# Eight PSUM banks and six in front for the second products of a feed-forward layer

## The chip, the cores and the metric

One core of a Trainium2 chip runs the whole program as one launch. The metric is the device time of that launch in microseconds. The engines are TensorE (PE, with its weight loads as PEld), VectorE (DVE), ScalarE (ACT), GpSimd (POOL) and SyncE (SP, which issues most of the DMAs).

## The reference, cut to what matters

Attention in a window, then a mixture of eight experts over all tokens, then one feed-forward layer. The change touches the last of these:

```python
def _moe2_ref(x, w_in, w_out):              # x 2304 x 512, w_in 512 x 2048, w_out 2048 x 512
    h = x @ w_in
    g = np.where(h >= 1, h, np.where(h <= -1, 0.0, (h + 1) ** 2 / 4))
    return g @ w_out
```

## The kernel before

Each fp32 product is made of three matmuls on a high and a low part of both factors (`mm3`, lines 76 to 78). The feed-forward layer is done with Strassen's scheme: seven block products in place of eight, for both matrix products.

The tokens go in three phases of 768. In each phase the 2048 inner columns go in eight units of 256, two units at a time. For a pair (i, i+1) the program first runs `g1` for both units and then one call of `g2s`.

`g1` makes the seven first products of a unit in four PSUM tiles with the tags a, b, c and d (one buffer each). Its last piece of work is a list of steps, `put7`, on ACT, DVE and POOL: it applies the activation g to the four quarters c22, f11, c21 and c12 of the result, forms the sums s13 and s24 of them (POOL, lines 726 to 732), and splits the seven blocks into `hh` (high, ACT, line 705) and `hl` (low, DVE, line 708). The blocks are numbered 0 to 6 in this order: c22, f11, c12, the two of s13 (3, 4), the two of s24 (5, 6). One step of every open list is given out at each "tick", so the order of the instructions in each engine's queue is the order in which the ticks gave them out, and each engine works its queue off in that order. The steps of the second unit's put7 are still being given out while g2s runs.

`g2s` makes the seven second products for three 128-token tiles: 21 results of 128 x 256. Two results share one PSUM bank (2 KB), so there are eleven "banks" of work, 0 to 10, block by block (bank 0 holds block 0 of tiles 0 and 1, bank 3 block 2 of tiles 0 and 1, bank 10 block 6 of tile 2). Each gets a first part from unit i and a second part from unit i+1. A full part is 6 matmuls, that of bank 10 is 3, so a call has 126. After its second part a bank is drained: in the first pair of a phase ACT copies it into the accumulator `acf` (line 842), in the others DVE adds it there (line 844). A tick comes after every third result part. The last call of the program takes the banks in another order, which starts with the blocks 0 and 1 and has blocks 5 of tile 0 in its bank 5.

The banks rotate through four PSUM buffers, which have the tag g2. Four first parts go in front; then come the second part of bank 0, the second part of bank 1, the first part of bank 4, the second part of bank 2, the first part of bank 5, and so on. The order is written out by the loop at the end of g2s:

```python
for b in range(4):
    yield from bank(b, 0)
for b in range(len(banks)):
    yield from bank(b, 1)
    drain(b)
    if 1 <= b < len(banks) - 3:
        yield from bank(b + 3, 0)
```

Behind the last call the three tiles are combined and stored (`combine`, lines 805 and 800, and lines 850 and 854).

Of the kernel before, what the change touches and what calls it, by code (L numbers as in the profile page):

```python
# [11 lines left out]
F32 = mybir.dt.float32  # L12
# [7 lines left out]
P = 128  # L20
# [9 lines left out]
def attn_moe_ffn(ctx: ExitStack, tc, q, k, v, w_gate, w1, w2, w_in, w_out, out):  # L30
# [10 lines left out]
    FU = 2 * P  # L41
# [33 lines left out]
    def mm3(ps, lh, ll, rh, rl, first, last, on=False):  # L75
        nc.tensor.matmul(ps, lhsT=lh, rhs=rh, start=first, stop=False, skip_group_check=on)  # L76
        nc.tensor.matmul(ps, lhsT=lh, rhs=rl, start=False, stop=False, skip_group_check=on)  # L77
        nc.tensor.matmul(ps, lhsT=ll, rhs=rh, start=False, stop=last, skip_group_check=on)  # L78
# [498 lines left out]
    def is_first(i):  # L577
        return i == 0 or units[i][:2] != units[i - 1][:2]

    def is_last(i):  # L580
        return i == NU - 1 or units[i][:2] != units[i + 1][:2]
# [207 lines left out]

    BLOCK = (6, 0, 1, 3, 5, 4, 2)  # L790
    NB = TH // P

    def combine(t, ns, acc, engines):

        n0, n1 = ns[0], ns[-1] + 1
        a = [acc[:, n0:n1, s, :] for s in range(7)]

        def put(s, r, x):
            rows_ = t * TP + r * TH
            nc.sync.dma_start(out=out[rows_ + n0 * P:rows_ + n1 * P, x * FU:(x + 1) * FU].rearrange("(n p) d -> p n d", p=P),  # L800
                              in_=a[s])

        for n, (o, x, z) in enumerate(((5, 1, None), (0, 4, None), (3, 5, None), (2, 1, (0, 0)), (6, 3, (0, 1)),
                                       (0, 5, (1, 0)), (3, 4, (1, 1)))):
            engines[n % len(engines)].tensor_tensor(a[o], a[o], a[x], ALU.add)
            if z is not None:
                put(o, *z)
            yield

    def g2s(i, acc, psp):  # L810

        kind, t, e, j = units[i]
        ops = [[*HT.pop(u), *W2.pop(u)] for u in (i, i + 1)]
        first, last = is_first(i), is_last(i + 1)
        end = i + 2 == NU
        flat = acc.rearrange("p n s d -> p (n s) d")
        if end:
            order = [(0, 0), (0, 1), (1, 0), (1, 1), (0, 2), (1, 2), (0, 3), (0, 4), (1, 3), (1, 4), (0, 5), (0, 6),
                     (1, 5), (1, 6), (2, 0), (2, 1), (2, 3), (2, 5), (2, 2), (2, 4), (2, 6)]
        else:  # L820
            order = [(n, s) for s in range(7) for n in range(NB)]
        banks = [sorted(order[x:x + 2]) for x in range(0, len(order), 2)]
        PS = {}
        count = [0]

        def part(b, x, u):
            if x == 0 and u == 0:
                PS[b] = psp.tile([P, 2, FU], F32, tag="g2", bufs=4, name="psg2")
            n, s = banks[b][x]
            hh, hl, wh, wl = ops[u]  # L830
            ts = slice(n * P, (n + 1) * P)
            mm3(PS[b][:, x], hh[:, s, ts], hl[:, s, ts], wh[:, BLOCK[s]], wl[:, BLOCK[s]], u == 0 and x == 0, u == 1,
                True)
            count[0] += 1
            return count[0] % 3 == 0

        def drain(b):
            f = [n * 7 + s for n, s in banks[b]]
            a = flat[:, f[0]:f[-1] + 1:max(f[-1] - f[0], 1)]
            ps = PS.pop(b)[:, 0:len(f)]  # L840
            if first:
                nc.scalar.activation(a, ps, AF.Copy)
            else:
                nc.vector.tensor_tensor(a, ps, a, ALU.add)  # L844

        V, G = nc.vector, nc.gpsimd
        n2 = [acc[:, NB - 1, s, :] for s in range(7)]

        def add(eng, o, x):
            eng.tensor_tensor(n2[o], n2[o], n2[x], ALU.add)  # L850

        def store(s, r, x):
            r0 = t * TP + r * TH + (NB - 1) * P
            nc.sync.dma_start(out=out[r0:r0 + P, x * FU:(x + 1) * FU], in_=n2[s])

        def bank(b, u):
            for x in range(len(banks[b])):
                if part(b, x, u):
                    yield

        for b in range(4):
            yield from bank(b, 0)
        for b in range(len(banks)):
            yield from bank(b, 1)
            drain(b)
            if 1 <= b < len(banks) - 3:
                yield from bank(b + 3, 0)
            if end:
                if b in (5, 6):
                    post.append(combine(t, [b - 5], acc, (V, G)))  # L870
                elif b == 8:
                    add(V, 5, 1)
                    add(V, 3, 5)
                    add(G, 6, 3)
                elif b == 9:
                    add(G, 0, 4)
                    add(G, 0, 5)
                    store(0, 1, 0)
                elif b == 10:
                    store(6, 0, 1)  # L880
                    add(V, 3, 4)
                    store(3, 1, 1)
                    add(V, 2, 1)
                    store(2, 0, 0)
        if last and not end:
            post.append(combine(t, list(range(NB)), acc, (V, G)))

# [79 lines left out]
    with tc.manual_schedule():  # L967
# [218 lines left out]
        for i in range(0, NU, 2):  # L1186
# [6 lines left out]
            if i and kind > units[i - 1][0]:  # L1193
# [4 lines left out]
                accp, hop, wp2 = (ctx.enter_context(tc.tile_pool(name=n, bufs=1)) for n in ("acf", "hpf", "w2f"))  # L1198
                acc = accp.tile([P, NB, 7, FU], F32, name="acf")
                pools["hop"] = hop  # L1200
# [20 lines left out]
            if kind == 0:  # L1221
                run(g2(i, acc, ps2, stg), False)
            else:
                run(g2s(i, acc, ps2), False)
                if i + 8 < NU and is_first(i):
                    side.append(sums(phase(i + 8)))
# [32 lines left out]
```

## Time and profile before

| | |
|---|---|
| three runs | 2120.49, 2121.81 and 2129.6 us; median 2121.81 |
| profiled execution | 2124.34 us, span 2122.6 |
| mean granted clock of PE | 0.988 of full speed |
| PE busy | 2051.3 us (97%) |
| DVE busy | 1342.4 us (63%) |
| ACT busy | 746.0 us (35%) |
| POOL busy | 727.2 us (34%) |
| DMA, mean over the span | 234 GB/s |

Matmuls overlap in the profile (the next starts before the last has ended), so a busy PE isn't PE at its peak; how densely they start says more. The feed-forward layer fills the last 420 us or so of the span, with twelve calls of g2s.

### The profile page before, as it was taken

The numbers are of one execution on the slowest core, as the hardware profiler recorded it, in microseconds if no ns is written. First come the engines' busy times: TensorE is split into PE (matmuls) and PEld (weight loads), VectorE is DVE, ScalarE is ACT, GpSimd is POOL, SyncE is SP. The second block draws the span as 40 slices with busy tenths as digits, with TensorE's granted clock in tenths as the row PEclk, the third lists the DMA queues.
The fourth block names the chain that finished last, engine by engine and source line by source line (L and its number), as shares of the span: only waits on it lengthen the run. The fifth ranks groups of instructions, "written<-read, shape, count | busy, mean of one in ns | idle before, by whom it ended". The sixth has DMA issues, their size and how long they took to land.

```text
span 2122.6 us, 32070 instructions
## 1 busy us (share of the span) xinstructions
PE 2051.3 (97%) x11719; PEld 1869.4 (88%) x11719; DVE 1342.4 (63%) x2967; ACT 746.0 (35%) x1716; POOL 727.2 (34%) x755
## 2 busy tenths in 40 slices
PE   7999999999999999999999999999999999898987
PEld 5888888998999898999899888899899889898987
DVE  5766655554555756666667656666666566858676
ACT  5767343333333331221122221121122263555542
POOL 4333346666756401112111011111110045646333
PEclk9999999999999999999999999999999999999998
DMA  7333568776777787676677597676675685775852
GB/s 152 82 86 96 196 222 328 246 263 247 254 252 258 261 324 260 235 258 230 237 266 249 192 339 244 232 275 226 229 273 208 224 315 197 307 280 208 320 196 100
DMA packets 238797, 496.91 MB, mean 234 GB/s; under 512 B 70704, under 2 KB 152624, under 8 KB 238640
## 3 DMA queue, kind: packets, MB, share of 16 engines
q1 hardware_dynamic: 222640, 475.34, 63.5%
q10 hardware_dynamic: 16000, 19.53, 3.0%
q8 instruction: 92, 1.51, 0.3%
q14 instruction: 65, 0.53, 0.1%
HBM read 353.39 MB, written 141.03 MB: 233 GB/s over the span
## 4 chain that ended last, share of the span: by engine, by line
PE 82%; DVE 6%; ACT 5%; DMA 4%; issue 1%; SPq 1%; POOL 0%; DVEq 0%; ACTq 0%; POOLq 0%
PE psg L76 15%; PE psg L78 14%; PE psg L77 14%; PE psc L76 3%; PE psd L76 3%; PE psc L77 3%; PE psc L78 3%; PE psd L77 3%; PE psd L78 3%; PE psb L76 2%; PE psb L78 2%; PE psb L77 2%; PE psa L77 2%; PE psa L78 2%; PE psa L76 2%; PE pso L375 2%
## 5 line engine op out<-in xcount | busy, mean ns | idle before, releaser
L76 PE MATMUL psg<-w2h,hh 128*128 128x512 f32 (+1 forms) x1584 | 574.5, 363 | 38.5 <-DVE acf L844 28.2
L78 PE MATMUL psg<-w2h,hl 128*128 128x512 f32 (+1 forms) x1584 | 571.2, 361 | 0.1
L77 PE MATMUL psg<-w2l,hh 128*128 128x512 f32 (+1 forms) x1584 | 570.9, 360 | 0.2 <-DMA w2l<-wd2l 0.2
L76 PEld LDWEIGHTS psg<-w2h,hh 128*128 128x128 f32 x1584 | 307.3, 194 | 82.5 <-DVE acf L844 30.4
L912 DVE SCALAR_TENSOR_TENSOR acc<-psg,pt,acc 128x512 f32<-128x512 f32 x252 | 187.8, 749 | 253.5 <-PE psg L78 252.0
L78 PEld LDWEIGHTS psg<-w2h,hl 128*128 128x128 f32 x1584 | 306.9, 194 | 42.9 <-DVE hl L708 0.5
L77 PEld LDWEIGHTS psg<-w2l,hh 128*128 128x128 f32 x1584 | 307.5, 194 | 40.4 <-DMA w2l<-wd2l 0.4
L684 ACT ACTIVATE hh<-c 128x384 fp32r<-128x384 f32 x270 | 140.8, 521 | 90.4 <-DVE c L779 53.9
L686 DVE SCALAR_TENSOR_TENSOR hl<-c,hh 128x384 fp32r<-128x384 f32 x270 | 164.0, 640 | 0.0
L751 ACT ACTIVATE p<-psa 128x384 f32<-128x384 f32 x57 | 28.0, 491 | 381.8 <-PE psa L78 353.0
L76 PE MATMUL psd<-sh,w1h 128*128 128x384 f32 x456 | 154.5, 339 | 2.2 <-DVE c L767 1.7
L78 PE MATMUL psd<-sh,w1l 128*128 128x384 f32 x456 | 153.4, 336 | 0.0
L77 PE MATMUL psd<-sl,w1h 128*128 128x384 f32 x456 | 153.3, 336 | 0.0
L192 POOL TENSOR_TENSOR t<-e 128x128 f32<-128x128 f32 x32 | 15.1, 471 | 380.4 <-DVE e L168 380.4
L193 POOL TENSOR_TENSOR t<-e,t 128x128 f32<-128x128 f32 x32 | 15.5, 484 | 324.2 <-DVE e L168 324.2
L726 POOL TENSOR_TENSOR s<-c,c 128x384 f32<-128x384 f32 x24 | 30.3, 1263 | 270.0 <-DVE c L702 270.0
L82 POOL TENSOR_TENSOR w2l<-raw,w2h 128x512 fp32r<-128x512 f32 x60 | 81.7, 1383 | 116.6 <-ACT w2h L81 116.6
L343 POOL TENSOR_TENSOR s<-s,mx 128x512 f32<-128x512 f32 (+2 forms) x80 | 66.6, 848 | 124.4 <-DVE mx L341 67.5
L76 PE MATMUL psc<-x0h,w1h 128*128 128x384 f32 x272 | 92.8, 341 | 2.3 <-DVE u L764 2.3
L761 DVE TENSOR_TENSOR u<-psb,p 128x384 f32<-128x384 f32 x57 | 31.7, 556 | 99.8 <-PE psb L78 79.6
L78 PE MATMUL psc<-x0h,w1l 128*128 128x384 f32 x272 | 92.4, 340 | 0.0
L77 PE MATMUL psc<-x0l,w1h 128*128 128x384 f32 x272 | 92.4, 340 | 0.0
(273 smaller groups left out, 4742.8 us busy)
## 6 DMA issues: line engine op xcount, KB each, us to landing
w1h<-wd1h SPq DMA_DIRECT2D x84, 896.0 KB, 4.8
w1l<-wd1l SPq DMA_DIRECT2D x84, 896.0 KB, 7.5
raw<-in_moe_w SPq DMA_DIRECT2D x60, 512.0 KB, 4.5
w2h<-wd2h SPq DMA_DIRECT2D x60, 512.0 KB, 5.4
w2l<-wd2l SPq DMA_DIRECT2D x60, 512.0 KB, 6.3
wd1h<-w1h SPq DMA_DIRECT2D x30, 896.0 KB, 6.2
wd1l<-w1l SPq DMA_DIRECT2D x30, 896.0 KB, 6.5
w2h<-wd2h SPq DMA_DIRECT2D x28, 896.0 KB, 7.2
```

Source lines behind the costliest of these rows:

```text
L76: nc.tensor.matmul(ps, lhsT=lh, rhs=rh, start=first, stop=False, skip_group_check=on)
L77: nc.tensor.matmul(ps, lhsT=lh, rhs=rl, start=False, stop=False, skip_group_check=on)
L78: nc.tensor.matmul(ps, lhsT=ll, rhs=rh, start=False, stop=last, skip_group_check=on)
L82: eng.tensor_tensor(l, x, h.bitcast(F32), ALU.subtract)
L343: nc.gpsimd.tensor_tensor(s[:, 0:nj, :nk], s[:, 0:nj, :nk], mx[:, 6:6 + nj].unsqueeze(2).to_broadcast([P, nj, nk]), ALU.mult)
L375: nc.tensor.matmul(PS[hs, x, :nq], lhsT=nat[b, "v", kb][:n, (2 * hp + j) * D:(2 * hp + j + 1) * D], rhs=at[:n, c, 0, TAIL[j]] if i == FULL ...
L684: nc.scalar.activation(h, c, AF.Relu)
L686: V.scalar_tensor_tensor(l, c, 0.0, h.bitcast(F32), ALU.max, ALU.subtract)
L726: G.tensor_tensor(s13[:, 0], c21, c22, ALU.add)
L751: nc.scalar.activation(p1, pa, AF.Copy)
L761: V.tensor_tensor(u2, pb, p1, ALU.add)
L912: nc.vector.scalar_tensor_tensor(a, ps, sc, a, ALU.mult, ALU.add)
```

## The change

The banks 4 to 7 of a call now take the tags a, b, c and d, which g1 uses before and after; the banks 0 to 3 and 8 to 10 keep the four buffers of g2. So the eleven banks rotate through all eight PSUM banks. Six first parts go in front in place of four, and the first part of bank b + 6 follows the second part of bank b from b = 0 on.

```diff
     NB = TH // P
+    AHEAD = 6
...
             if x == 0 and u == 0:
-                PS[b] = psp.tile([P, 2, FU], F32, tag="g2", bufs=4, name="psg2")
+                tag = {"tag": "abcd"[b - 4]} if 4 <= b < 8 else {"tag": "g2", "bufs": 4}
+                PS[b] = psp.tile([P, 2, FU], F32, name="psg2", **tag)
...
-        for b in range(4):
+        for b in range(AHEAD):
             yield from bank(b, 0)
         for b in range(len(banks)):
             yield from bank(b, 1)
             drain(b)
-            if 1 <= b < len(banks) - 3:
-                yield from bank(b + 3, 0)
+            if b + AHEAD < len(banks):
+                yield from bank(b + AHEAD, 0)
```

PE's queue in the second pair of the first phase: `psg_17952` is bank 0, `psg_17959` bank 1, `psg_18019` bank 4 (before). The rows begin in the second part of bank 1.

```order
L78 MATMUL psg_17959<-w2h,hl 128x256
L76 MATMUL psg_17959<-w2h,hh 128x256
L77 MATMUL psg_17959<-w2l,hh 128x256
L78 MATMUL psg_17959<-w2h,hl 128x256
L76 MATMUL psg_18019<-w2h,hh 128x256
L77 MATMUL psg_18019<-w2l,hh 128x256
```

With the change `psg_18010` is bank 5, `psg_18026` bank 6. The rows begin at the end of bank 5's first part.

```order
L77 MATMUL psg_18010<-w2l,hh 128x256
L78 MATMUL psg_18010<-w2h,hl 128x256
L76 MATMUL psg_17952<-w2h,hh 128x256
L77 MATMUL psg_17952<-w2l,hh 128x256
L78 MATMUL psg_17952<-w2h,hl 128x256
L76 MATMUL psg_17952<-w2h,hh 128x256
```

Before, the first part of bank 4, which takes the buffer of bank 0, was the seventh part and followed two second parts; with the change bank 5's first part stands ahead of the first second part, and the first bank that takes the buffer of bank 0 is bank 8, the eleventh part.

DVE's queue in the same call, from the hl of the first unit's s24 on (`s_17838`); `s_17925` and `s_17926` are s13 and s24 of the second unit, `c_17923` is its c12. Before:

```order
L708 TENSOR_TENSOR hl<-s_17838,hh 128x768
L708 TENSOR_TENSOR hl<-c_17923,hh 128x384
L844 TENSOR_TENSOR acf<-psg_17952,acf 128x2x256
L844 TENSOR_TENSOR acf<-psg_17959,acf 128x2x256
L708 TENSOR_TENSOR hl<-s_17925,hh 128x768
L844 TENSOR_TENSOR acf<-psg_17976,acf 128x2x256
L844 TENSOR_TENSOR acf<-psg_17993,acf 128x2x256
L708 TENSOR_TENSOR hl<-s_17926,hh 128x768
L844 TENSOR_TENSOR acf<-psg_18019,acf 128x2x256
```

With the change (line 846 is the drain that was line 844):

```order
L708 TENSOR_TENSOR hl<-s_17838,hh 128x768
L708 TENSOR_TENSOR hl<-c_17923,hh 128x384
L846 TENSOR_TENSOR acf<-psg_17952,acf 128x2x256
L708 TENSOR_TENSOR hl<-s_17925,hh 128x768
L846 TENSOR_TENSOR acf<-psg_17959,acf 128x2x256
L708 TENSOR_TENSOR hl<-s_17926,hh 128x768
L846 TENSOR_TENSOR acf<-psg_17976,acf 128x2x256
L846 TENSOR_TENSOR acf<-psg_17993,acf 128x2x256
```

The two hl of the second unit's sums moved forward: one drain stands ahead of the first of them in place of two, and two ahead of the second in place of four.

ACT's queue in the first call of the first phase, where ACT drains; `s_17216` and `s_17217` are the second unit's sums. Before:

```order
L705 ACTIVATE hh<-c_17214 128x384
L842 ACTIVATE acf<-psg_17243 128x2x256
L705 ACTIVATE hh<-s_17216 128x768
L842 ACTIVATE acf<-psg_17250 128x2x256
L842 ACTIVATE acf<-psg_17267 128x2x256
L705 ACTIVATE hh<-s_17217 128x768
L842 ACTIVATE acf<-psg_17283 128x2x256
```

With the change:

```order
L705 ACTIVATE hh<-c_17214 128x384
L705 ACTIVATE hh<-s_17216 128x768
L844 ACTIVATE acf<-psg_17243 128x2x256
L705 ACTIVATE hh<-s_17217 128x768
L844 ACTIVATE acf<-psg_17250 128x2x256
L844 ACTIVATE acf<-psg_17267 128x2x256
```

Here too the hh of both sums moved forward, and the drains of banks 1 and 2 now stand behind the hh of s24.

## Rows read from the trace of the kernel before

**Rows 1.** Waits of PE, 1700 us to the end: total us, times, longest.

```profile
PE psg L76 <- DVE acf L844: 28.2, 9, 3.2
PE psg L76 <- ACT acf L842: 7.0, 4, 2.6
```

**Rows 2.** Windows in one ordinary call: length, engines' busy time (instructions), PEclk, DMA share.

```profile
core 0: us, PE busy (x) PEld busy (x) DVE busy (x) ACT busy (x) POOL busy (x), PEclk, DMA share, GB/s
1740.88:1745.20 4.32, 4.32 (x37) 4.27 (x36) 3.93 (x8) 3.99 (x8) 1.49 (x2) 1.00 0.78 267
...
1749.00:1751.40 2.40, 2.40 (x13) 2.40 (x13) 1.62 (x2) 0.85 (x1) 2.40 (x2) 0.50 0.00 0
```

**Rows 3.** Window of the g1 pair ahead of that call.

```profile
1726.17:1740.88 14.71, 14.71 (x86) 14.71 (x85) 9.53 (x17) 9.60 (x19) 5.21 (x4) 1.00 0.92 368
```

**Rows 4.** Windows of the eight ordinary calls of g2s, two of them and the sum.

```profile
1740.88:1761.01 20.13, 16.96 (x127) 16.59 (x127) 15.72 (x22) 7.59 (x13) 16.26 (x16) 0.92 0.29 99
...
1916.00:1934.50 18.50, 15.38 (x128) 15.18 (x128) 15.05 (x22) 6.49 (x11) 13.27 (x12) 1.00 0.31 107
...
sum 159.64, PE 134.34 PEld 132.34 DVE 123.22 ACT 58.37 POOL 95.26; mean PE 16.79 PEld 16.54 DVE 15.40 ACT 7.30 POOL 11.91
```

**Rows 5.** Windows of the three calls that open a phase, two and the sum.

```profile
1708.70:1726.17 17.47, 15.61 (x127) 15.21 (x127) 9.19 (x12) 11.45 (x21) 5.63 (x5) 1.00 0.79 314
1848.00:1866.42 18.42, 15.70 (x127) 15.26 (x127) 9.01 (x13) 12.26 (x23) 6.23 (x5) 1.00 1.04 398
...
sum 55.71, PE 48.40 PEld 47.15 DVE 27.27 ACT 36.02 POOL 18.08; mean PE 16.13 PEld 15.72 DVE 9.09 ACT 12.01 POOL 6.03
```

**Rows 6.** Windows of the last call and of what follows it.

```profile
2089.45:2110.67 21.22, 18.29 (x127) 17.85 (x126) 16.22 (x25) 6.54 (x11) 7.18 (x7) 0.84 0.00 1
2110.67:2122.60 11.93, 0.16 (x2) 0.00 (x0) 6.95 (x11) 0.00 (x0) 5.82 (x7) 0.62 0.40 132
```

**Rows 7.** Timeline of PE: start, duration, line, idle time before and releaser.

```profile
1748.52 0.58 PE L76 MATMUL psg<-w2h,hh 128*128 128x256 f32 x1 [3.17 <-DVE acf L844]
```

**Rows 8.** Timeline of DVE in the same call (T = 1740.88).

```profile
1742.96 0.55 DVE L719 TENSOR_TENSOR c<-psd,u 128x384 f32<-128x384 f32 x1
...
1745.65 1.74 DVE L708 TENSOR_TENSOR hl<-s,hh 128x768 fp32r<-128x768 f32 x1
1747.32 0.55 DVE L708 TENSOR_TENSOR hl<-c,hh 128x384 fp32r<-128x384 f32 x1
1747.79 1.27 DVE L844 TENSOR_TENSOR acf<-psg,acf 128x512 f32<-128x512 f32 x2
1748.99 1.64 DVE L708 TENSOR_TENSOR hl<-s,hh 128x768 fp32r<-128x768 f32 x1
```

**Rows 9.** DMA issues, 1700 us to the end: count, KB each, median us to landing.

```profile
w2h<-wd2h SPq DMA_DIRECT2D x26, 896.0 KB, 7.2
```

**Rows 10.** Timeline of POOL and ACT in the same call.

```profile
1748.80 1.01 POOL L732 TENSOR_TENSOR s<-c,s 128x384 f32<-128x384 f32 x1
...
1749.84 0.85 ACT L705 ACTIVATE hh<-s 128x768 fp32r<-128x768 f32 x1 [2.38 <-POOL s L732]
```

**Rows 11.** Line 708, 1700 us to the end: ns min/median/max, first and last start.

```profile
L708 DVE TENSOR_TENSOR hl<-s,hh x48: 948/1518/1766, 1706.9 to 2103.2; 128x768 fp32r<-128x768 f32 x48
```

**Rows 12.** Timeline of PE and ACT, first two phase-opening calls (T = 1708.70, 1848.00).

```profile
1714.58 0.39 PE L76 MATMUL psg<-w2h,hh 128*128 128x256 f32 x1 [1.41 <-ACT acf L842]
...
1718.22 0.84 ACT L705 ACTIVATE hh<-s 128x768 fp32r<-128x768 f32 x1 [1.31 <-POOL s L732]
...
1719.60 0.39 PE L76 MATMUL psg<-w2h,hh 128*128 128x256 f32 x1 [0.45 <-ACT acf L842]
...
1854.88 0.60 ACT L842 ACTIVATE acf<-psg 128x512 f32<-128x512 f32 x1 [0.93 <-DMA out<-acf]
...
1858.13 0.84 ACT L705 ACTIVATE hh<-s 128x768 fp32r<-128x768 f32 x1 [0.27 <-POOL s L732]
```

**Rows 13.** Timeline of DVE and SP, the last call (T = 2089.45) and its tail.

```profile
2094.23 1.74 DVE L708 TENSOR_TENSOR hl<-s,hh 128x768 fp32r<-128x768 f32 x1
...
2116.72 3.36 SPq L800 DMA_DIRECT2D out<-acf  x7
```

## The prediction

> **What bounds the kernel now.** I read the waits of TensorE (PE) first, then the stretches of the feed-forward second products as windows, then the timeline of one pair of units on every engine that PE waits for.
>
> PE is nearly always busy, so a gain has to come from its few waits or from its clock. The waits [rows 1] show one kind that repeats: the first matmul of a psg bank waits 9 times for a DVE drain (28.2 us) and 4 times for an ACT drain (7.0 us). That is 35.2 us, all in twelve calls of g2s. I write T for the start of a call. A call is 126 matmuls of 256 columns. They run at 0.12 us each: 36 of them fill the 4.32 us of the first window of [rows 2]. So a call needs 126 x 0.12 = 15.12 us, and the g1 pair ahead of it takes 14.71 us [rows 3].
>
> The windows show what the calls take: 159.64 us for the eight ordinary ones [rows 4], 55.71 for the three that open a token phase, whose drains are ACT's [rows 5], 21.22 for the last [rows 6]. That is 236.57 against 12 x 15.12 = 181.4: 55.1 us over. It has two parts. One is the wait itself, in the sample pair 3.17 us [rows 7]. The other is the clock: after that wait PE runs for a while at a granted clock of 0.50, that is 1.2 instead of 2.4 GHz [rows 2]; a matmul then takes 256/1.2 = 0.213 us, 0.093 more. The ordinary call that kept its clock took 18.50 us, 3.4 over the floor, which is wait and restart; its sister at 0.92 took 20.13 [rows 4]. So a wait of some 3 us costs about 1.5 us more in clock, mostly.
>
> Why the wait is there is seen in DVE's timeline [rows 8]. Bank 4's first part needs the buffer of bank 0. Bank 0 was complete in PE at about T+3.6, but its drain stands in DVE behind hl of the first unit's sums (1.74 us, from T+4.77) and hl of c12, and so runs at T+6.9, together with the next drain. DVE is not short of time overall; the order in its queue makes the drain late.
>
> **The change part by part.** No instruction is added or taken away; matmuls, drains, loads and stores are the same, in another order.
>
> *Banks 4 to 7 take tags a to d.* Their old readers are the second unit's put7. The last of them reads d by T+2.63 (L719 in [rows 8]), and a is free long before. PE asks for a at T+2.88, b at T+3.60, c at T+5.04, d at T+6.48. No wait, even if that latest reader stood for all: the least cover is then 0.25 us. On the other side the next g1 writes a to d from T+15 on, when drains 4 to 7 are some 3 us old: nothing.
>
> *Six banks ahead.* PE now does the 36 matmuls of six first parts (0.72 us each part), then bank 0's second part (done T+5.04), bank 6, bank 1's second part, bank 7, bank 2's second part, and asks for the buffer of bank 0 (as bank 8) only at T+7.92. Before it asked at T+4.32. Bank 7 reads hl of the first unit's sums at T+7.08; DVE has it at T+6.5. Weights come no later: w2 of the first unit is freed earlier in the call, w2 of the second is first read 1.44 us later; its transfer takes 7 us [rows 9] under a g1 pair of 14.71. POOL's and SP's work keeps its order; the saturated DMA of the g1 stretch (0.92 in [rows 3]) rests in most of the call.
>
> *What is late next.* Four more parts make one more tick before drain 0, so hl of the second unit's sums (s13) moves from behind drain 1 to between drains 0 and 1, and that of s24 to between drains 1 and 2. By the durations of [rows 8]: drain 0 runs T+6.99 to 7.60 (0.32 us ahead of need), hl of s13 takes 1.6 to T+9.2, drain 1 ends at T+9.85. PE wants that buffer for bank 9 at T+9.36 and waits 0.5. hl of s24 can't start before ACT's hh, which ends at T+9.8 and follows POOL's s24 [rows 10]; it takes 0.95 to 1.75 us [rows 11], and drain 2 ends at T+11.4 to 12.2. Bank 10 wants it at about T+11.45: a wait of 0 to 0.8, say 0.5. With 0.1 for each restart a call takes 15.12 + 1.1 = 16.2. If hl is short each time (DVE beside an idle POOL) both waits nearly vanish: 15.4. Both are below the 1.41 us that left the clock alone in the first phase-opening call (clock 1.00 in [rows 5], and another 0.45 there [rows 12]), so I take no clock loss.
>
> Sum for the eight: 159.64 - 8 x 16.2 = 30.0 us.
>
> *The three calls that open a phase.* Here ACT drains, and drain 1 now stands behind hh of s24, which ACT starts at T+9.52 in the first and T+10.13 in the second [rows 12], waiting for POOL. It takes 0.84, the drain 0.6, so bank 9, wanted at T+9.36, starts at T+10.9 or T+11.5: waits of 1.5 and 2.15, plus restart. The calls take 16.7 and 17.4, the third like the second. Drain 0 of the second waits for stores of the phase before, until T+6.88 [rows 12]; bank 8 asks a microsecond after. 55.71 - 51.5 = 4.2 us.
>
> *The last call* has its banks in another order: bank 5 already needs block 5 of the first unit, whose hl ends at T+6.5 [rows 13], and is now asked for it at T+3.84. A new wait of 2.65 us, plus 0.1, and by the windows of [rows 4] some 1.0 of clock: 18.9. Gain 2.3. Behind it the tail (11.93 us in [rows 6]) is a chain of DVE adds and SP stores. DVE has 6.95 us of work in it. The last drains come closer together in PE (0.72 us apart, a drain takes 0.61), so the adds between them are pushed behind PE's end: about 1 us more. SP, which issues the stores at 0.48 us each and now ends 9.4 us after PE [rows 13], stays the last, with one store more among the late ones: 0 to +0.5 us. I take 0.
>
> In all 30.0 + 4.2 + 2.3 = 36.5 us. The profiled execution took 2124.34 us (span 2122.6 and 1.74 around it), 2.53 more than the median of the runs, 2121.81. From the median: 2085.3; I say 2085.5.
>
> **A rule that speaks against it.** On the row: after 1.41 us and again 0.45 us of waiting, 4 us apart, the window still has clock 1.00 [rows 5, 12]. The Trainium skill, "TensorE: Matmul & The Clock Gate", section "A second HAM failure mode: psum-queue depth-cycling", tells of a kernel that cycles through PSUM banks, where short idle gaps between groups make the clock swing between its levels. By that rule the two small waits of each call would cost clock too; the trace so far doesn't bear it out. What it would make is case 2 below.
>
> **The rivals**, with the likeliest as case 1.
> 1. *The likeliest*: as above, gain 30 to 42 us. Chance 0.72.
> 2. *The small waits cost the clock.* If each of the eleven calls but the last loses the 1.5 us that a lost clock costs now, 16.5 us go: gain 20, 2102. If the clock stays low from bank 9 to the end of the call (48 matmuls x 0.093 = 4.5 us), eight calls lose 36 and nothing is won. For it: an ordinary call at 0.92 and the last at 0.84 [rows 4, 6]. Against: these waited some 3 us at once. Chance 0.14, a third of it within 0.5% of no change.
> 3. *All is hidden.* With hl at 0.95 each time both waits go: 8 x 0.8 more, and the last call keeps its clock: gain 44, 2078. Against: POOL is busy for 95 of the 160 us of these stretches [rows 4], and the median of these hl is 1.5 [rows 11]. Chance 0.08.
> 4. *Slower: drains 1 to 10 stand behind the chain POOL s24, ACT hh, DVE hl.* Before, four drains had passed ahead of the last hl; now only two. Each microsecond that s24 ends later is one of PE in each of eleven calls. It ends 8.9 us after T now [rows 10]. 36.5/11 = 3.3 us later nothing is won; at 4.5 us later it is 13 us more: 2135. For that POOL would need other work ahead of s24; its order of instructions is unchanged. Chance 0.03.
> 5. *Nothing happens*, because PE meets another wait of 3 us at bank 8. Drain 0 has 0.32 us of cover; it would need three. Chance 0.03.
>
> **How the numbers follow.** About 0.5% (10.6 us) is what a measurement of this kernel tells from no change. Faster: cases 1 and 3 and two thirds of case 2: 0.72 + 0.08 + 0.09 = 0.89. Slower 0.03; the rest, 0.08, is the same. The range: low end 2074 from case 3 with the phase-opening calls a little shorter too; high end 2103 from case 2 at its milder price.
>
> **What would show it.** Right: the wait of PE for the drains at bank 4 gone; windows of ordinary calls 15.4 to 16.6 us at clock 1.00; waits of about half a microsecond at banks 9 and 10; about 2 us at bank 9 in phase-opening calls, for ACT; a wait for hl in the last call; g1 stretches still 14.71. Wrong: windows of ordinary calls above 18 us, a granted clock under 0.95 in them, a wait at bank 7 for hl or at bank 4 to 7 for put7's reads, or g1 stretches that grow by what the calls lose.

## The result, and the profile after

The changed kernel took 2090.86 us (median of four runs, 2088.37 to 2092.15) against 2121.24 before (four runs, 2120.49 to 2129.6): ratio 0.9847, interval 0.9820 to 0.9873. Four more runs beside another set of the kernel before gave 2091.65 and 0.9849 (0.9833 to 0.9866). The forecast was 2085.5 in 2074 to 2103. The profiled execution took 2092.15 us, 32.2 less than that of before.

Waits of PE on the psg banks from 1700 us to the end: total us, times, longest.

```profile
PE psg L76 <- DVE acf L846: 9.9, 8, 1.8
PE psg L76 <- ACT acf L844: 4.4, 3, 1.5
PE psg L78 <- DVE hl L708: 1.9, 3, 1.4
PE psg L76 <- ACT hh L705: 1.0, 1, 1.0
```

The drains (DVE's now line 846, ACT's 844) cost 14.3 us in place of the 35.2 of [rows 1], and there are two new kinds: waits for `hl` and for `hh`.

Windows of the changed kernel: three of the eight ordinary calls and the sum of all eight, two of the three calls that open a phase and their sum, the last call and the tail; the columns are those of [rows 2].

```profile
1740.11:1756.64 16.53, 15.48 (x127) 15.21 (x127) 14.61 (x22) 7.34 (x13) 12.66 (x12) 1.00 0.48 170
...
1802.59:1821.38 18.79, 16.99 (x128) 16.71 (x127) 15.34 (x22) 8.63 (x14) 13.27 (x9) 0.91 0.67 249
...
1932.20:1949.44 17.24, 15.44 (x128) 15.21 (x127) 15.29 (x22) 8.61 (x14) 12.63 (x9) 1.00 0.45 159
...
sum 135.08, PE 125.16 PEld 123.17 DVE 118.14 ACT 58.01 POOL 87.88; mean PE 15.65 PEld 15.40 DVE 14.77 ACT 7.25 POOL 10.99
...
1708.61:1725.40 16.79, 15.37 (x128) 15.17 (x127) 9.22 (x12) 11.58 (x21) 5.65 (x5) 1.00 0.98 385
1837.56:1854.97 17.41, 15.62 (x127) 15.22 (x127) 9.76 (x13) 12.15 (x23) 6.27 (x5) 1.00 1.04 412
...
sum 51.60, PE 46.60 PEld 45.59 DVE 28.73 ACT 35.88 POOL 18.19; mean PE 15.54 PEld 15.20 DVE 9.58 ACT 11.96 POOL 6.06
...
2060.53:2078.47 17.94, 15.63 (x127) 15.18 (x126) 14.75 (x23) 6.53 (x11) 6.55 (x7) 1.00 0.00 1
2078.47:2090.40 11.93, 0.16 (x2) 0.00 (x0) 7.69 (x13) 0.00 (x0) 5.82 (x7) 0.70 0.40 132
```

The twelve calls take 135.08 + 51.60 + 17.94 = 204.62 us, 31.95 less than the 236.57 of before: the whole gain of the profiled execution is in them. Six of the eight ordinary calls take 16.47 to 16.53 us at clock 1.00. The other two (18.79 and 17.24) are the third ordinary call of the first and of the second phase. The g1 pair between two calls takes 14.71 us as in [rows 3], and the tail 11.93 as in [rows 6].

Timeline of the changed kernel in the call at T = 1740.11 (PE at banks 9 and 10, DVE, POOL, ACT) and in the call at 1802.59 (DVE, POOL, PE): start, duration, instruction, in brackets the idle time before it and who ended it.

```profile
1749.48 0.39 PE L76 MATMUL psg<-w2h,hh 128*128 128x256 f32 x1
1749.70 0.28 PE L77 MATMUL psg<-w2l,hh 128*128 128x256 f32 x1
...
1750.90 0.28 PE L78 MATMUL psg<-w2h,hl 128*128 128x256 f32 x1
1752.23 0.39 PE L76 MATMUL psg<-w2h,hh 128*128 128x256 f32 x1 [1.05 <-DVE acf L846]
1752.45 0.28 PE L77 MATMUL psg<-w2l,hh 128*128 128x256 f32 x1
...
1747.06 0.68 DVE L846 TENSOR_TENSOR acf<-psg,acf 128x512 f32<-128x512 f32 x1
1747.65 1.17 DVE L708 TENSOR_TENSOR hl<-s,hh 128x768 fp32r<-128x768 f32 x1
1748.75 0.68 DVE L846 TENSOR_TENSOR acf<-psg,acf 128x512 f32<-128x512 f32 x1
1750.61 0.96 DVE L708 TENSOR_TENSOR hl<-s,hh 128x768 fp32r<-128x768 f32 x1 [1.19 <-ACT hh L705]
1751.49 1.88 DVE L846 TENSOR_TENSOR acf<-psg,acf 128x512 f32<-128x512 f32 x3
...
1748.09 1.61 POOL L732 TENSOR_TENSOR s<-c,s 128x384 f32<-128x384 f32 x1
...
1749.73 0.85 ACT L705 ACTIVATE hh<-s 128x768 fp32r<-128x768 f32 x1 [3.01 <-POOL s L732]
...
1813.11 1.71 DVE L708 TENSOR_TENSOR hl<-s,hh 128x768 fp32r<-128x768 f32 x1 [1.18 <-ACT hh L705]
...
1812.16 1.84 POOL L82 TENSOR_TENSOR sl<-st,sh 128x768 fp32r<-128x768 f32 x1
...
1815.47 0.39 PE L76 MATMUL psg<-w2h,hh 128*128 128x256 f32 x1 [1.80 <-DVE acf L846]
```

Read it as a chain. POOL's last step of s24 ends at 1749.70, ACT's hh follows it to 1750.58, DVE has been idle for 1.19 us when it can start hl at 1750.61, and drains 2 to 4 stand behind that hl. PE wants the buffer of bank 2 for bank 10 and gets it at 1752.23, at T+12.12. The call keeps the order of things but not the durations of before: hl of s13 took 1.17 us (1.64 in [rows 8]) and POOL's step 1.61 (1.01 in [rows 10]). In the call at 1802.59 hl of s24 runs into POOL's line 82, takes 1.71 in place of 0.96, and the wait is 1.80.

One caution for what follows. The first call of g2s starts at 1708.70 us before and at 1708.61 after (1708.18 in a second profile of it), but at 1701.73 to 1706.74 in the seven other kernels, although nothing ahead of it was changed. It is not one event: the same instruction of PE starts at 75.74 to 80.61 us in the ten profiles, and further steps of 2 to 3 us follow near 800, 1100 and 1300 us. The runs of one kernel can lie as far apart (2065.33 to 2072.34 for e2_ahead5 below). Why stays open. So I compare the calls' lengths, and the medians only where they differ by more than these 7 us.

### The profile page after: what moved, and what is told of

It reads as the page before. It is cut to its first block, busy times and chain, and to the rows that moved or that the text cites. A ratio compares the mean times of both kernels' runs of the same rounds, so it can differ in the third digit from the quotient of the medians.

```text
span 2090.4 us, 32070 instructions
## 1 busy us (share of the span) xinstructions
PE 2033.1 (97%) x11719; PEld 1853.3 (89%) x11719; DVE 1333.3 (64%) x2967; ACT 745.3 (36%) x1716; POOL 730.2 (35%) x755
## 3 DMA queue, kind: packets, MB, share of 16 engines
q8 instruction: 92, 1.51, 0.3%
## 4 chain that ended last, share of the span: by engine, by line
PE 80%; DVE 7%; ACT 7%; DMA 2%; issue 2%; POOL 1%; SPq 1%; ACTq 0%; DVEq 0%; POOLq 0%
PE psg L76 14%; PE psg L78 14%; PE psg L77 14%; PE psc L76 3%; PE psc L77 3%; PE psc L78 3%; PE psd L76 3%; PE psd L77 3%; PE psd L78 3%; PE psa L77 2%; PE psa L78 2%; PE psb L76 2%; PE psb L78 2%; PE psb L77 2%; PE psa L76 2%; ACT g L698 2%
## 5 line engine op out<-in xcount | busy, mean ns | idle before, releaser
L76 PE MATMUL psg<-w2h,hh 128*128 128x512 f32 (+1 forms) x1584 | 568.1, 359 | 20.0 <-DVE acf L846 9.9
L78 PE MATMUL psg<-w2h,hl 128*128 128x512 f32 (+1 forms) x1584 | 565.2, 357 | 1.9 <-DVE hl L708 1.9
L77 PE MATMUL psg<-w2l,hh 128*128 128x512 f32 (+1 forms) x1584 | 564.7, 356 | 0.0
L76 PEld LDWEIGHTS psg<-w2h,hh 128*128 128x128 f32 x1584 | 300.6, 190 | 64.0 <-DVE acf L846 11.5
L78 PEld LDWEIGHTS psg<-w2h,hl 128*128 128x128 f32 x1584 | 300.6, 190 | 45.1 <-DVE hl L708 2.5
L77 PEld LDWEIGHTS psg<-w2l,hh 128*128 128x128 f32 x1584 | 300.8, 190 | 40.2
```

## The experiments

Theory A: the wait of before came from the buffer of bank 0, held by a drain that stands late in DVE's queue; what waits now is again a matter of which bank asks when, and what stands ahead of its drain. Theory B: the six parts in front matter for another reason, because second parts would otherwise wait for `hl` of the sums. Theory C: what is left is the chain POOL s24, ACT hh, DVE hl itself. Diffs are against the changed kernel; "calls" is the sum of the twelve windows of the profiled execution, "ordinary" one ordinary call.

| run | banks, parts in front | median us (lowest to highest; before: its three medians) | ratio to before (interval) | calls us | ordinary us |
|---|---|---|---|---|---|
| before | 4, 4 | 2121.24 to 2123.62 | 1 | 236.57 | 18.50 to 21.10 |
| e7_five_banks | 5, 4 | 2095.01 (2090.75 to 2097.01) | 0.9866 (0.9849 to 0.9882) | 211.54 | 17.16 to 18.62 |
| e1_banks_only | 8, 4, old order | 2084.68 (2082.86 to 2087.52) | 0.9817 (0.9803 to 0.9832) | 201.93 | 16.84 to 16.93 |
| e6_ahead4 | 8, 4 | 2076.95 (2075.99 to 2077.91) | 0.9783 (0.9768 to 0.9799) | 193.53 | 16.14 to 16.22 |
| e2_ahead5 | 8, 5 | 2068.02 (2065.33 to 2072.34) | 0.9740 (0.9720 to 0.9759) | 183.74 | 15.11 |
| r_after (the change again) | 8, 6 | 2091.65 (2088.85 to 2094.92) | 0.9849 (0.9833 to 0.9866) | 207.47 | 16.48 to 18.74 |
| e3_ahead7 | 8, 7 | 2097.58 (2096.36 to 2100.63) | 0.9882 (0.9864 to 0.9899) | 214.04 | 17.31 to 18.87 |
| e4_late_s24 | 8, 6, s24 3 ticks later | 2085.66 (2082.18 to 2086.86) | 0.9817 (0.9799 to 0.9834) | 199.30 | 15.18 to 21.43 |
| e8_late2 | 8, 6, s24 2 ticks later | 2070.49 (2067.63 to 2072.78) | 0.9749 (0.9731 to 0.9766) | 187.53 | 15.17 to 15.25 |

**The change again.** 

> The changed kernel again, beside the experiments on the same chip. 2091 us, within 3; ordinary calls of g2s 16.5 us with one wait of 1.05 us at bank 10.

The six short ordinary calls repeat within 0.05 us, and both third ones again wait 1.80; here both lost the clock (18.74 and 18.71). The last call took 19.25.

**The banks alone**, with the old order of parts.

```diff
-        for b in range(AHEAD):
+        for b in range(4):
...
-            if b + AHEAD < len(banks):
-                yield from bank(b + AHEAD, 0)
+            if 1 <= b < len(banks) - 3:
+                yield from bank(b + 3, 0)
```

> All eight banks, but the order of the parts as before (four in front). Theory A (the wait before came from the buffer alone: bank 4 wanted the buffer of bank 0, whose drain stood behind hl in DVE's queue): the wait at bank 4 is gone here too; small waits for hl of the second unit appear (0.3 us at bank 3's second part, 0.7 at bank 4's), ordinary calls 16.0 to 16.6 us, phase-opening calls 15.5 to 16.5, time 2085 to 2093. Theory B (six in front is what helps, since the second parts come before the second unit's hl is ready): with four in front PE waits 2 us and more for hl, ordinary calls 17.5 to 19, time 2103 to 2115.

Its waits of PE, then the timeline of DVE, POOL and PE in the call at T = 1732.18.

```profile
PE psg L78 <- DVE hl L708: 13.2, 21, 1.1
...
1739.13 1.28 DVE L846 TENSOR_TENSOR acf<-psg,acf 128x512 f32<-128x512 f32 x2
1740.33 1.66 DVE L708 TENSOR_TENSOR hl<-s,hh 128x768 fp32r<-128x768 f32 x1
...
1740.16 1.01 POOL L732 TENSOR_TENSOR s<-c,s 128x384 f32<-128x384 f32 x1
...
1742.04 0.38 PE L78 MATMUL psg<-w2h,hl 128*128 128x256 f32 x1 [1.08 <-DVE hl L708]
```

No wait for a drain is left, so theory A is right about the buffer. Theory B's wait exists too: block 3 of bank 4's second part needs hl of s13, which stands behind two drains and ends at 1741.99. It is worth 1.08 us a call and not the 2 or more that would have made the six parts necessary. It is still more than the 0.7 expected, so the calls (16.84 to 16.93) lie above the expected 16.0 to 16.6. The banks alone give all that the whole change gives: 201.93 us of calls against 204.62 and 207.47. The six parts in front added nothing.

**Five banks**: the old order, by the loop of the run before this one, and only bank 4 moved (tag a).

```diff
-                tag = {"tag": "abcd"[b - 4]} if 4 <= b < 8 else {"tag": "g2", "bufs": 4}
+                tag = {"tag": "a"} if b == 4 else {"tag": "g2", "bufs": 4}
```

> Order of the parts as before, but five buffers: bank 4 takes tag a, the banks 5 to 10 rotate with the others through the four of g2. Theory A: drain 0 ends at T+7.6 whatever PE does; bank 5 is the first that wants it, at T+5.8, and waits 1.7 to 1.9 us where bank 4 waited 3.2; ordinary calls 17.0 to 17.6 where the clock holds; time 2090 to 2103. Rival: one bank more is no help, since the wait is for DVE being busy and only moves: bank 5 waits 2.8 us and more, calls as before, time over 2112.

Two of its ordinary calls as windows, and PE's wait in the first.

```profile
1735.98:1753.38 17.40, 15.62 (x127) 15.21 (x127) 15.49 (x22) 7.58 (x13) 13.54 (x13) 1.00 0.33 113
1768.09:1786.71 18.62, 16.85 (x127) 16.65 (x127) 15.58 (x22) 6.53 (x11) 13.35 (x12) 0.91 0.30 106
...
1743.66 0.39 PE L76 MATMUL psg<-w2h,hh 128*128 128x256 f32 x1 [1.77 <-DVE acf L846]
```

The wait moves from bank 4 to bank 5 and ends at T+7.68, when drain 0 is done: it shrinks from 3.17 [rows 7] to 1.70 to 1.79, by the two parts (1.44 us) that bank 5 stands further back. This is the size of the cause that the prediction read off [rows 8]. Four of the eight calls lost their clock after such a wait, four did not.

**Five parts in front.**

```diff
-    AHEAD = 6
+    AHEAD = 5
```

> Eight banks, five parts in front. Drain 2 stands ahead of hl of s24 again in DVE's queue, and bank 10 asks for its buffer 0.7 us later. Theory A (what is left of the wait is drain 2's place in DVE's queue): no wait at bank 10, ordinary calls 15.1 to 15.5 us, time 2069 to 2075. Theory C (what is left is the chain POOL s24, ACT hh, DVE hl itself, and PE would wait for that hl at bank 7's second part instead): ordinary calls stay at 16.2 to 16.6, time 2087 to 2092.

Its waits of PE on g2s, the sum of its eight ordinary windows, and DVE in the call at T = 1731.79.

```profile
PE psg L78 <- DVE hl L708: 1.4, 1, 1.4
PE psg L76 <- ACT hh L705: 0.2, 1, 0.2
...
sum 120.88, PE 120.88 PEld 120.88 DVE 112.96 ACT 56.35 POOL 78.95; mean PE 15.11 PEld 15.11 DVE 14.12 ACT 7.04 POOL 9.87
...
1740.41 1.27 DVE L846 TENSOR_TENSOR acf<-psg,acf 128x512 f32<-128x512 f32 x2
1742.28 0.96 DVE L708 TENSOR_TENSOR hl<-s,hh 128x768 fp32r<-128x768 f32 x1 [0.60 <-ACT hh L705]
```

Every ordinary call is at its floor: 8 x 15.11 us, PE busy all through. One part fewer in front does two things: banks 8 to 10 ask 0.72 us later, and drain 2 stands ahead of hl of s24 (two drains in the row at 1740.41), so no bank waits for that chain any more. Theory C falls as a limit: the chain is as long as before and costs nothing. It has the shortest calls of all, and its median is 23.6 us under that of the changed kernel beside the same runs of before, 1 us under what was expected. That e8_late2 below is 2.5 us slower is within the caution above.

**Four and seven parts in front**, each first part right behind the second part of the bank that lies so many earlier.

```diff
-    AHEAD = 6
+    AHEAD = 4
```

```diff
-    AHEAD = 6
+    AHEAD = 7
```

> Eight banks, four parts in front, and the first part of bank b + 4 right behind the second part of bank b. Theory A by the queues: hl of the second unit's s13 stands behind drains 0 and 1 and ends at T+9.4 to 9.8; bank 4's second part wants it at T+9.2 to 9.3: a wait of 0.2 to 0.6 in ordinary calls, 15.4 to 15.9 us, no wait for a drain; time 2070 to 2078. Rival: four in front is as bad as in the run with the old order, whose order in DVE is nearly the same: a wait of about 1.1 us for hl, 16.4 to 16.9, time 2080 to 2086.

> Eight banks, seven parts in front. One more tick ahead of drain 0 puts hl of s13 ahead of drain 0 and hl of s24 ahead of drain 2 in DVE's queue. Theory A: bank 8 wants drain 0 at T+7.2 to 7.4 and gets it at T+8.8, a wait of 1.2 to 1.6 us, and bank 10 waits again 0.3 to 1.1; ordinary calls 16.9 to 18, time 2092 to 2106, so slower than six. Rival (the more in front, the better): 15.1 to 16.3, time under 2088.

First DVE and PE with four in front (call at T = 1734.45), then with seven (T = 1737.42), and there the window of one call that lost its clock.

```profile
1742.59 1.68 DVE L708 TENSOR_TENSOR hl<-s,hh 128x768 fp32r<-128x768 f32 x1
...
1744.32 0.39 PE L78 MATMUL psg<-w2h,hl 128*128 128x256 f32 x1 [0.84 <-DVE hl L708]
```

```profile
1744.37 1.77 DVE L708 TENSOR_TENSOR hl<-s,hh 128x768 fp32r<-128x768 f32 x1
1746.07 1.27 DVE L846 TENSOR_TENSOR acf<-psg,acf 128x512 f32<-128x512 f32 x2
...
1746.80 0.39 PE L76 MATMUL psg<-w2h,hh 128*128 128x256 f32 x1 [1.32 <-DVE acf L846]
...
1933.13:1951.93 18.80, 17.09 (x127) 16.68 (x127) 15.53 (x22) 8.59 (x14) 12.59 (x9) 0.91 0.45 164
```

Too few in front, and the second parts catch up with hl of s13 (0.77 to 0.84 us, more than the 0.2 to 0.6 expected, so calls of 16.14 to 16.22 in place of 15.4 to 15.9); too many, and hl of s13 moves ahead of drain 0 in DVE's queue, so that bank 8 waits 1.30 to 1.32. With seven, bank 7 of the ordinary calls also waits 0.39 to 0.46 for the first unit's hl, which was not expected, and the wait expected at bank 10 came in one call only (0.34). So both sides of the best number are explained by theories A and B together. With seven in front, two of the eight calls (18.80 and 18.87) lost their clock, with the same two waits as the others.

**s24 of the second unit later**, with six in front: its hh and hl are given out three ticks, or two, behind hl of s13.

```diff
-            for _ in range(3 if i % 2 == 0 else 0):
+            for _ in range(3):
```

```diff
-            for _ in range(3 if i % 2 == 0 else 0):
+            for _ in range(3 if i % 2 == 0 else 2):
```

> The changed kernel with the split (hh, hl) of the second unit's s24 given out three ticks later, as it is for the first unit; DVE then has drains 0 to 3 ahead of that hl, ACT drains 0 to 2 ahead of that hh. Theory A: no wait at bank 10 and, in the phase-opening calls, none at bank 9 (1.5 us now); ordinary calls 15.1 to 15.5, phase-opening ones 15.2 to 15.7, time 2069 to 2075. Theory C: the waits move to bank 7's second part, for hl; time 2087 to 2092.

> Six in front, the split of the second unit's s24 two ticks later instead of three. DVE's order is that of the run with three ticks, but on ACT hh of s24 now stands ahead of both copies of line 551, which wait for POOL's sums. Theory A with this cause of the new wait: the waits of 2.9 us for hh in the first ordinary call of two phases are gone, ordinary calls all 15.1 to 15.4, time 2070 to 2077. Rival: the three-tick run's wait came from the later place itself, and a shorter one of 1.5 to 2.5 us stays; time 2078 to 2083.

With three ticks, ACT and PE in the first ordinary call (T = 1736.56):

```profile
1751.02 0.52 ACT L551 ACTIVATE x0h<-st 128x384 fp32r<-128x384 f32 x1 [7.83 <-POOL st L544]
1751.45 0.83 ACT L705 ACTIVATE hh<-s 128x768 fp32r<-128x768 f32 x1
...
1752.33 0.54 PE L76 MATMUL psg<-w2h,hh 128*128 128x256 f32 x1 [2.88 <-ACT hh L705]
```

The waits at bank 10 in the ordinary calls and at bank 9 in those that open a phase went, but the expected 2069 to 2075 was missed, by a cause that I had not seen. Three ticks later hh of s24 stands behind the next tokens' `x0h` (line 551) in ACT's queue, and that one waits 7.83 us for POOL sums. Where line 551 is in the way, in the first ordinary call of two phases, the call takes 21.43 and 20.82 us. With two ticks hh stands ahead of it. ACT in the first ordinary call (T = 1735.24):

```profile
1744.87 0.85 ACT L705 ACTIVATE hh<-s 128x768 fp32r<-128x768 f32 x1 [3.00 <-POOL s L732]
1750.54 0.53 ACT L551 ACTIVATE x0h<-st 128x384 fp32r<-128x384 f32 x1 [4.82 <-POOL st L544]
```

All ordinary calls take 15.17 to 15.25, and 2070.49 lies at the lower end of what was expected. The cause was the place in ACT's queue.

## Why the prediction came out right, and which term was off

*What bounds and why* (bank 4 waits for a drain that DVE's order makes late): right, shown by e1_banks_only, where the wait is gone with nothing but more banks, and sized by e7_five_banks.

*Banks 4 to 7 on the tags a to d cost nothing*: right. No wait at these banks for a reader of put7; the g1 pair still takes 14.71.

*The eight ordinary calls, forecast 8 x 16.2 = 129.6*: 135.08. This is the mis-sized term, 5.5 us short of the gain. Six calls are 0.27 to 0.33 us over, together 1.85; the two third ones are 2.6 and 1.0 over, together 3.6. Three sizes in it were wrong.

- The wait at bank 9 (0.5) did not come, since hl of s13 took 1.17 and not 1.6: drain 1 ended at T+9.32, when bank 9 asked. So PE asked for bank 10's buffer at about T+10.9 and not at T+11.45, and all of the waiting fell there: 1.05 in place of twice 0.5. That the sum came out is partly luck. Drain 2 ended at about T+12.1, and the forecast stands for T+11.95. POOL's s24 took 1.61 and not the 1.01 of [rows 10], and so ended at T+9.59 in place of T+8.93; but the hl behind it took 0.96, where the forecast leaves room for 1.5. The two errors nearly cancel.
- A restart was put at 0.1, and the sum counts one for two waits: by its own figures it is 15.12 + 1.0 + 0.2 = 16.3. A restart costs more than that. From the row at 1750.90 to the one at 1752.23 the starts lie 1.33 us apart, then 0.22; in a full stream each step is 0.12. So a wait shown as 1.05 costs 1.21 + 0.10 = 1.31, which is 0.26 more than the wait: the profile counts idle time from the end of the matmul before. With 0.1 for bank 9, whose first step is 0.22 as well (1749.48 to 1749.70), the call comes out: 15.12 + 1.31 + 0.1 = 16.53. So does e6_ahead4: 15.12 + 0.84 + 0.26 = 16.22.
- hl of s24 had its bound of 1.75 in the prediction, but I took one value for all calls. In the third ordinary call of two phases it takes 1.71, because POOL's line 82 is under way; the wait is 1.80, and there the clock can go: granted clock 0.91 at 1802.59, 1.00 at 1932.20.

The durations in the first and the third have one cause, shown by rows of all runs: `hl` on DVE and the s-steps on POOL don't run side by side. In the profiles of the change (twice) and of the seven other kernels there are 213 pairs in which POOL's line 732 and an hl of 768 columns overlap. The one that starts later ends 0.81 to 0.89 us after the one that started first, in all 213. Where DVE is first (185 pairs) line 732 takes 1.6 us; where POOL is first (28) it takes 1.01 and hl, in all but one of them, 1.64 to 1.68, as before in [rows 8, 10]. The change moved hl of s13 one drain forward, in front of POOL's step, and so turned the order round: DVE became shorter, and POOL, which is on the chain, longer. I carried over both durations, and wrote that POOL's order of instructions is unchanged; it is, but not its order against DVE. The Trainium skill, "SBUF — State Buffer", section "Who interferes with whom", says that a DVE instruction with two inputs in SBUF and a GpSimd instruction that reads SBUF take turns, and that the order of issue decides which of them waits. The rows agree: 1.01 against 1.61 us for the same POOL instruction.

*The three calls that open a phase*, forecast 16.7, 17.4 and 17.4: 16.79, 17.41 and 17.40. Bank 9 started at T+10.93 and T+11.54 (forecast T+10.9 and T+11.5). In the second and third there was one small wait more, 0.28 us for hl at bank 7, and the one at bank 9 was shorter for it (1.50 and not 2.15).

*The last call*, forecast 18.9 with a wait of 2.65 for hl: 17.94. It waited 0.95 for hh and 1.36 for hl and kept its clock in this execution (1.00); in the second profile of the same kernel it lost it and took 19.25. The forecast lies between the two, so that it is near either is luck. In the three other kernels with this pair of waits (0.94 or 0.95, then 1.36 or 1.37) the last call kept its clock in e3_ahead7 and lost it in the two with s24 later. *The tail*, forecast unchanged: 11.93 and 11.93.

The sum: 36.5 - 5.5 (ordinary) - 0.1 (opening) + 1.0 (last) = 31.9, against 31.95 in the windows.

*The rivals.* Small waits that cost the clock: not the ones forecast. (The two of before that the prediction puts 4 us apart lie 4.6 us apart.) Six ordinary calls with a wait of 1.05 each, and three opening ones with 1.42 to 1.50, stayed at 1.00. The rule on cycling through PSUM banks in the Trainium skill, "TensorE: Matmul & The Clock Gate", section "A second HAM failure mode: psum-queue depth-cycling", did not show here at this size. A loss of the clock does show a little further on, and no run tells whether that is this rule's. After waits of 1.70 to 1.80 us, three of the four such calls in the two profiles of the change and four of eight with five banks ran at about 0.91; after the pair of 0.4 and 1.3 us with seven in front, two of eight did. So the rival was nearer than its 0.14 looks, and a call that loses its clock pays 1.2 to 1.6 us. All is hidden: not with six in front, but with five it is. The chain POOL s24, ACT hh, DVE hl: this rival named the place of what is left. s24 did end 0.66 us later, and yet the calls at full clock are only 0.3 over the forecast, since the hl behind it was short; 3.3 us would have been needed for no gain. Nothing happens: excluded by the drain waits, 35.2 to 14.3 us.

*The signs.* Of the signs that the prediction named for being right, the windows of 15.4 to 16.6 us came in six of the eight ordinary calls, the half microseconds at banks 9 and 10 in none. Two of those for being wrong came in small: one ordinary call above 18 us with a clock of 0.91, and the wait at bank 7 for hl.

## What to carry to other kernels

With a rotation of buffers, count for each bank when it asks and what stands ahead of its drain in the queue of the draining engine; the number of banks alone doesn't decide. Here eight banks with four, five, six and seven parts in front took 2077, 2068, 2091 and 2098 us, since each part more in front moves an hl past a drain. When instructions change their order against another engine, take the durations of before only for instructions that don't share a resource, and try the distance by one in each direction: it costs one constant. A step given out later can land behind one that waits for something else, as hh did behind `x0h` (7.83 us of idle time on ACT).

## What the runs showed of the hardware that was not expected

A DVE subtraction and a POOL subtraction, both with two inputs in SBUF, took turns in 213 of 213 overlapping pairs; whichever came second paid (POOL 1.61 us in place of 1.01, DVE 1.64 to 1.68 in place of 0.96, but for one pair). A wait of PE between matmuls of 256 columns costs 0.26 us more than the profile shows for it, at the full clock. And the clock after a wait of 1.70 to 1.80 us is not the same from call to call of one execution: 7 of 12 such calls lost it (18.62 against 17.40 us in e7_five_banks). By and large the share grows with the wait: none of 28 ordinary calls whose longest wait was 0.77 to 1.09 us lost it and none of nine opening calls with one of 1.42 to 1.51, but seven of the eight ordinary calls of before, with 3.12 to 3.19. Out of line are the two of eight with seven in front, whose longest wait was 1.30 to 1.32. What tells calls with the same wait apart stays open.
